# A fused windowed-attention and PReLU kernel: the mask of four head pairs added by TensorE, and slices y and h moved ahead in the first token tile

## The chip, the cores and the metric

The kernel runs on one core of one Trainium2 chip. The metric is the device time of one execution, in microseconds (us). Before the change the median of three runs is 894.59 us (893.28 to 896.59).

## The reference

Windowed causal attention over 8 batches of 8 heads, 576 positions, 64 dims a head (heads 0 to 3 with a plain window of 32, heads 4 to 7 with every fourth key of 128), whose output is 4608 tokens of 512 features; then a feed-forward layer with a PReLU:

```python
scores = scale * np.matmul(q, k.transpose(0, 1, 3, 2))
scores = np.where(masks[None, :, :, :], scores, -1000000000.0)
scores = scores - np.max(scores, axis=-1, keepdims=True)
attn = np.exp(scores)
attn = attn / (np.sum(attn, axis=-1, keepdims=True) + 1e-09)
x = np.matmul(attn, v).transpose(0, 2, 1, 3).reshape(4608, 512)
h = x @ w_in                                   # 512 x 2048
g = np.maximum(h, 0.0) + alpha * np.minimum(h, 0.0)
return g @ w_out                               # 2048 x 512
```

## The kernel before, in words

**Attention.** Two heads are one `Pair`; pair p is batch p // 4, heads 2(p % 4) and the next. A pair goes through `scores` (72 small products on TensorE into two PSUM banks of 5 and 4 blocks of 64 keys), `maxima` (VectorE, twice: scale and add the mask into SBUF at L194, reduce to the negative maximum at L197), `exponentials` (ScalarE, nine of 128x64 at L204, from SBUF, each with its sum), `divisions` and `turns` (VectorE: sum, reciprocal, product, 32x32 transposes into `pt`, L211 to L219), `values` (76 small products, L232, into two banks `o`), and `highs` (ScalarE) and `lows` (VectorE), which write `o` as a rounded part and a remainder into `x`.

**Feed-forward.** Each factor is kept as a high and a low part, and each term is three products of 128x128 by 128x512: high by high, high by low, low by high (weight part first). `ffn_h` of a slice f of 128 of the 2048 columns is 12 products into one bank `h` (L341). `ffn_relu` (ScalarE, L349 and L350) takes both halves of the PReLU, `ffn_sum` (VectorE, L355) joins them, `ffn_high` (ScalarE, L368) and `ffn_low` (VectorE, L373) split the result g, and `ffn_y` is 12 products into four banks `y` (L388), three for each.

**Weights.** They arrive as 64-bit floats. A `Conversion` of one slice is a magnitude (ScalarE, L308), four word operations (VectorE, L314 to L320), a high part (ScalarE, L326) and a low part (VectorE, L329). The list `wq` sets the order of the slices ((0, f) is a slice of the first matrix, (1, f) of the second), and `taken` how many conversions are begun at the end of each step.

**Staging.** Pairs 0 to 3 make the first token tile (tile 0 is 512 tokens, all of batch 0 but 64); a start-up loop over s takes them and pair 4's scores. Then a loop over n = 0 to 5 runs the first six slices of tile 0 (called slice n below) beside pairs 5 to 7, and ends with tile 0's partial sums copied out of the y banks and stored (`ob`, L398 and L400). Tile 1's 16 slices follow (slice 6 is its first), then the rest of tile 0, tile 2, and a paired stage for the other tiles.

**What sets the order.** Nothing is scheduled by a planner: all five engines run what the program text says, in that order, so an instruction that waits holds up everything behind it on its engine. All loads and stores are issued by SP, in program order. Eight PSUM banks are handed out in turn: four, called a, for h, o and the scores of pairs from 5 on, and four, called y, for the scores of pairs 0 to 4 and then for y.

## Time and profile before

| | before |
|---|---|
| median of three runs | 894.59 us |
| profiled execution, device time | 895.02 us |
| its span | 892.9 us |
| TensorE busy | 853.4 us (96%) |
| VectorE / ScalarE / GpSimd busy | 561.3 / 394.3 / 46.9 us |
| granted TensorE clock, mean | 0.98 |

The profile is of one execution on the hardware. PE is TensorE, DVE VectorE, ACT ScalarE, POOL GpSimd, SP the engine that issues DMAs. A row of the timeline gives a start, a duration, engine, line, operation, `out<-in` by the program's names with partitions x elements, and in brackets the engine's idle time just before, with what ended it. The profile leaves buffer numbers out, so that all pairs, slices and weights have like names and are told apart by their place in the engine's order. PEclk is the granted clock as a share of full speed.

### The profile page before, as it was taken

To read this page: it belongs to the slowest core of one execution; us is meant where nothing else is said; L and a number is where in the kernel's file an instruction comes from. 1 tells how busy PE (TensorE), PEld (TensorE's weight loads), DVE (VectorE), ACT (ScalarE), POOL (GpSimd) and SP (SyncE) were. 2 spreads that over 40 slices of the span, in tenths; PEclk is the share of its full clock that TensorE was granted. 3 is DMA by queue.
4 is the path that set the end of the run, shared out by engine and by line. 5 is a ranking of instruction groups with operands and counts; after the bars stand their busy time and mean duration, and the time that the engine had idled before them with its cause. 6 is when DMAs were issued, how large, how long until landed. Compare 5 with 4: busy or idle time off the path is not lost.

```text
span 892.9 us, 19710 instructions
## 1 busy us (share of the span) xinstructions
PE 853.4 (96%) x8048; PEld 706.5 (79%) x8048; DVE 561.3 (63%) x964; ACT 394.3 (44%) x1118; POOL 46.9 (5%) x52
## 2 busy tenths in 40 slices
PE   4668999999999999999999999999999999999998
PEld 4556888888888788888888878888788888888886
DVE  6988799976767677675437655764366537304721
ACT  5566466542533444464336442653255226204600
POOL 0000000020223350000000000000000000000000
PEclk9669999999999999999999999999999999999999
DMA  9612245216889965565556555655365466436631
GB/s 344 219 59 94 86 151 174 80 47 193 253 273 334 301 201 175 188 190 162 156 166 193 173 178 174 195 162 162 96 192 158 148 179 194 124 98 172 180 128 47
DMA packets 101448, 151.81 MB, mean 170 GB/s; under 512 B 8432, under 2 KB 47344, under 8 KB 101360
## 3 DMA queue, kind: packets, MB, share of 16 engines
q1 hardware_dynamic: 101360, 150.58, 54.9%
q8 instruction: 63, 1.03, 0.5%
q14 instruction: 25, 0.20, 0.1%
HBM read 116.99 MB, written 33.55 MB: 169 GB/s over the span
## 4 chain that ended last, share of the span: by engine, by line
PE 94%; DVE 2%; issue 2%; ACT 1%; DMA 0%; SPq 0%; DVEq 0%; ACTq 0%
PE y L676 30%; PE h L341 15%; PE pA L538 15%; PE y L388 15%; PE pC L538 7%; PE o L232 5%; PE pB L538 4%; PE s L186 3%; ACT w_dt.float L204 1%; DMA ws<-w_in 0%; DVE pt L219 0%; DVE w_dt.float L213 0%; DVE w_dt.float32r L329 0%; DVE nm L197 0%; DVE wa L318 0%
## 5 line engine op out<-in xcount | busy, mean ns | idle before, releaser
L341 PE MATMUL h<-x,w_dt.float32r 128*128 128x512 f32 x576 | 144.4, 400 | 1.6 <-issue 1.6
L388 PE MATMUL y<-g,w_dt.float32r 128*128 128x512 f32 x576 | 138.4, 389 | 0.0
L341 PEld LDWEIGHTS h<-x,w_dt.float32r 128*128 128x128 f32 x576 | 109.6, 193 | 25.2 <-issue 1.8
L388 PEld LDWEIGHTS y<-g,w_dt.float32r 128*128 128x128 f32 x576 | 108.0, 188 | 22.5
L676 PE MATMUL y<-gp,ring_w 128*128 128x512 f32 x480 | 112.3, 390 | 0.0
L676 PEld LDWEIGHTS y<-gp,ring_w 128*128 128x128 f32 x480 | 89.7, 188 | 18.9
L676 PE MATMUL y<-gp,ring_xA 128*128 128x512 f32 x444 | 103.8, 390 | 0.0
L676 PEld LDWEIGHTS y<-gp,ring_xA 128*128 128x128 f32 x444 | 83.0, 188 | 17.5
L204 ACT ACTIVATE pr<-pr,nm 128x64 f32<-128x64 f32 x216 | 72.2, 336 | 47.2 <-DVE nm L197 47.2
L580 ACT COPY stage<-pA 128x512 f32<-128x512 f32 x72 | 42.3, 587 | 105.2 <-PE pA L538 105.2
L606 DVE TENSOR_TENSOR gp<-n,gp 128x512 fp32r<-128x512 f32 x96 | 63.1, 683 | 0.0
L368 ACT CAST g<-m 128x512 fp32r<-128x512 f32 x48 | 29.7, 619 | 75.4 <-DVE m L363 69.2
L598 DVE SCALAR_TENSOR_TENSOR n<-n,bal,stage 128x512 f32<-128x512 f32 x72 | 53.9, 748 | 13.6 <-ACT n L594 12.8
L538 PE MATMUL pA<-parts_w,ring_w 128*128 128x512 f32 x234 | 57.7, 390 | 0.7 <-ACT raw_xA L268 0.7
L602 ACT CAST gp<-n 128x512 fp32r<-128x512 f32 x96 | 56.6, 615 | 1.8 <-DVE n L598 1.8
L538 PE MATMUL pA<-parts_w,ring_xA 128*128 128x512 f32 x228 | 56.2, 390 | 0.5 <-ACT raw_xB L268 0.5
L676 PE MATMUL y<-gp,ring_g 128*128 128x512 f32 x228 | 54.5, 391 | 0.0
L699 DVE TENSOR_TENSOR ob<-y,py 128x512 f32<-128x512 f32 x24 | 16.4, 690 | 57.8 <-PE y L676 57.8
L538 PEld LDWEIGHTS pA<-parts_w,ring_w 128*128 128x128 f32 x234 | 43.9, 188 | 9.9 <-ACT raw_xA L268 0.8
L594 ACT ACTIVATE n<-stage 128x512 f32<-128x512 f32 x72 | 45.6, 633 | 12.5 <-DVE stage L587 11.9
L538 PEld LDWEIGHTS pA<-parts_w,ring_xA 128*128 128x128 f32 x228 | 42.7, 188 | 9.5 <-ACT raw_xB L268 0.6
L676 PEld LDWEIGHTS y<-gp,ring_g 128*128 128x128 f32 x228 | 42.5, 188 | 9.1
(97 smaller groups left out, 1147.3 us busy)
## 6 DMA issues: line engine op xcount, KB each, us to landing
ring_w<-wS SPq DMA_DIRECT2D x68, 256.0 KB, 2.9
ring_xA<-wS SPq DMA_DIRECT2D x67, 256.0 KB, 2.9
ring_w<-wO SPq DMA_DIRECT2D x40, 256.0 KB, 2.7
ring_xA<-wO SPq DMA_DIRECT2D x37, 256.0 KB, 2.7
out<-ob SPq DMA_DIRECT2D x36, 256.0 KB, 2.9
ring_g<-wS SPq DMA_DIRECT2D x33, 256.0 KB, 2.9
wO<-w_dt.float32r SPq DMA_DIRECT2D x32, 256.0 KB, 5.0
wS<-wc SPq DMA_DIRECT2D x16, 512.0 KB, 3.7
```

The source lines that it names most:

```text
L204: nc.scalar.activation(out=self.pr[:, r, :], in_=self.pr[:, r, :], func=AF.Exp, bias=self.nm[:, r:r + 1], scale=1.0, accum_out=self.sm[:, ...
L232: nc.tensor.matmul(self.po[u][e * D:(e + 1) * D, a:z, :], lhsT=self.v[rows, i, :], rhs=self.pt[rows, a * BK + (BQ if i else 0):z * BK - (B ...
L341: nc.tensor.matmul(ms[t, f], lhsT=weight(0, a, f)[:, c * P:(c + 1) * P], rhs=half(t, c)[:, e, :], start=(c == 0 and n == 0), stop=(c == NC ...
L368: nc.scalar.copy(out=g[:, 0, :], in_=ms[t, f])
L388: nc.tensor.matmul(ys[t][c], lhsT=weight(1, a, f)[:, c * P:(c + 1) * P], rhs=g[:, e, :], start=(first and n == 0), stop=(last and n == 2),)
L538: nc.tensor.matmul(to, lhsT=w[:, (2 * a + c) * P:(2 * a + c + 1) * P], rhs=part_of(name, e)[:, c * TT:(c + 1) * TT], start=start and c == ...
L580: nc.scalar.copy(out=self.s(n), in_=self.A)
L594: nc.scalar.activation(out=self.m[n], in_=self.at(n), func=AF.Relu, scale=-1.0)
L598: nc.vector.scalar_tensor_tensor(out=self.m[n], in0=self.m[n], scalar=bal[:, f:f + 1], in1=self.at(n), op0=ALU.mult, op1=ALU.add)
L602: nc.scalar.copy(out=self.g(n)[:, 0], in_=self.m[n])
L606: nc.vector.tensor_tensor(out=g[:, 1], in0=self.m.pop(n), in1=g[:, 0].bitcast(F32), op=ALU.subtract)
L676: nc.tensor.matmul(ys2[tt], lhsT=w[:, k * P:(k + 1) * P], rhs=g[:, e], start=j == 0 and n == 0, stop=j == GF - 1 and n == 2)
```

## The change

Three edits, in program order.

**The mask.** For pairs 1 to 4 the mask is added in PSUM: ahead of the 72 products of the scores TensorE multiplies a 128x128 identity (`unit_r`) by the mask (`added`, 320 and 256 columns), and the scores accumulate on top. L194 goes for these pairs; the maximum is reduced straight from PSUM and then scaled by a small `tensor_scalar_mul`, and the exponentials read PSUM and scale there. The identity is made by GpSimd at the program's start, and ScalarE casts it and the two masks.

**The weights.** Slice (0, 3) comes ahead of (1, 1), and of the loop's steps the first begins two conversions, where before the second did.

**The loop over n.** `ffn_y` of slice n - 1 and `ffn_h` of slice n + 2 come ahead of the pair's `values` (before: h of slice n + 1 behind them, y at the end of the step). The relus of slice n + 2 come directly behind g's high part, ahead of the exponentials, and its sum directly behind g's low part.

```diff
@@ -5,6 +5,7 @@
 import concourse.tile as tile
 from concourse import mybir
 from concourse._compat import with_exitstack
+from concourse.masks import make_identity
 
 F32 = mybir.dt.float32
 F32R = mybir.dt.float32r
@@ -120,6 +121,11 @@
     taken = 2 * S + vsize
     spare_pr = [rooms[i][:, taken:taken + HB * BK].rearrange("p (r k) -> p r k", r=HB) for i in range(2)]
     spare_a = [rooms[i][:, taken:taken + DM].bitcast(U32) for i in (2, 3)]
+    added_all = const.tile([P, NMASK + 2, BK], F32R, tag="xC0", name="added")
+    added = {kind: added_all[:, kind:kind + HB] for kind in (PLAIN, DILATED)}
+    unit_r = added_all[:, NMASK:].rearrange("p j k -> p (j k)")
+    unit = rooms[0][:, taken + HB * BK:taken + HB * BK + P]
+    make_identity(nc, unit)
 
 
     cells = {}
@@ -154,6 +160,7 @@
             self.id = f"{b}_{c}"
             self.pr = spare_pr[p % 2] if b < 2 else pr0
             self.room = rooms[c] if b < 2 else None
+            self.onto = 1 <= p <= NC
             self.sm = sums[p % 2]
 
         def load_qk(self):
@@ -177,6 +184,11 @@
 
 
             self.ps = [bank(self.banks, [P, n, BK], f"s_{self.id}_{i}") for i, n in enumerate((CUT0, HB - CUT0))]
+            if self.onto:
+                for i, (a, z) in enumerate(((0, CUT0), (CUT0, HB))):
+                    nc.tensor.matmul(
+                        self.ps[i], lhsT=unit_r, rhs=added[self.mask][:, a:z],
+                        start=True, stop=False, skip_group_check=True)
             for j in range(HB):
                 for u in range(2):
                     for e in range(2):
@@ -185,25 +197,30 @@
                             self.k[rows, None, :BQ].broadcast_to([D, 2, BQ]))
                         nc.tensor.matmul(
                             self.ps[j // CUT0][m * BQ:(m + 1) * BQ, j % CUT0, :], lhsT=self.q[rows, n * BQ:(n + 1) * BQ],
-                            rhs=keys, start=True, stop=True)
+                            rhs=keys, start=not self.onto, stop=True, skip_group_check=self.onto)
 
         def maxima(self, between=()):
             between = list(between)
             self.nm = sml.tile([P, HB], F32, tag="nm", name=f"nm_{self.id}")
             for i, (a, z) in enumerate(((0, CUT0), (CUT0, HB))):
-                nc.vector.scalar_tensor_tensor(
-                    out=self.pr[:, a:z], in0=self.ps[i], scalar=SCALE, in1=mask_sb[:, self.mask + a:self.mask + z],
-                    op0=ALU.mult, op1=ALU.add)
+                if not self.onto:
+                    nc.vector.scalar_tensor_tensor(
+                        out=self.pr[:, a:z], in0=self.ps[i], scalar=SCALE, in1=mask_sb[:, self.mask + a:self.mask + z],
+                        op0=ALU.mult, op1=ALU.add)
                 nc.vector.tensor_reduce(
-                    out=self.nm[:, a:z], in_=self.pr[:, a:z], axis=mybir.AxisListType.X, op=ALU.max, negate=True)
+                    out=self.nm[:, a:z], in_=self.ps[i] if self.onto else self.pr[:, a:z],
+                    axis=mybir.AxisListType.X, op=ALU.max, negate=True)
+                if self.onto:
+                    nc.vector.tensor_scalar_mul(self.nm[:, a:z], self.nm[:, a:z], SCALE)
             for op in between:
                 op()
 
         def exponentials(self, a=0, z=HB):
             for r in range(a, z):
                 nc.scalar.activation(
-                    out=self.pr[:, r, :], in_=self.pr[:, r, :], func=AF.Exp,
-                    bias=self.nm[:, r:r + 1], scale=1.0, accum_out=self.sm[:, r:r + 1],
+                    out=self.pr[:, r, :], in_=self.ps[r // CUT0][:, r % CUT0, :] if self.onto else self.pr[:, r, :],
+                    func=AF.Exp, bias=self.nm[:, r:r + 1], scale=SCALE if self.onto else 1.0,
+                    accum_out=self.sm[:, r:r + 1],
                 )
 
         def divisions(self):
@@ -770,8 +787,9 @@
 
 
     wq = [(0, 0), (0, 1), (1, 0)]
-    for f in range(1, NF):
-        wq += [(0, f + 1), (1, f)] if f + 1 < NF else [(1, f)]
+    wq += [(0, 2), (0, 3), (1, 1), (0, 4), (1, 2), (0, 5), (1, 3), (1, 4), (1, 5)]
+    for f in range(CUT, NF):
+        wq += [(0, f), (1, f)]
     order.update({w: i for i, w in enumerate(wq)})
     loads, convs = list(wq), list(wq)
 
@@ -804,8 +822,10 @@
     pairs[2].load_v()
     pairs[3].load_v()
     pairs[0].scores()
+    before = conversion()
+    nc.scalar.copy(out=unit_r, in_=unit)
+    nc.scalar.copy(out=added[PLAIN], in_=mask_sb[:, PLAIN:PLAIN + HB])
     pairs[1].scores()
-    before = conversion()
     for op in before.words():
         op()
     before.high()
@@ -833,6 +853,8 @@
             ffn_h(0, 0, 0, 2)
         u.turns()
         later = conversion()
+        if s == 0:
+            nc.scalar.copy(out=added[DILATED], in_=mask_sb[:, DILATED:DILATED + HB])
         if s + 2 <= NC:
             pairs[s + 2].scores()
         if s:
@@ -859,7 +881,7 @@
     load()
     late, now = [w], [conversion()]
 
-    taken = [1, 2, 1, 1, 1, 2] + [1, 1, 2, 1, 1, 1, 2, 1, 1, 2, 1, 2, 1]
+    taken = [2, 1, 1, 1, 1, 2] + [1, 1, 2, 1, 1, 1, 2, 1, 1, 2, 1, 2, 1]
 
     def ahead():
         while taken and len(convs) - taken[0] < len(loads):
@@ -869,29 +891,31 @@
         scored = pairs[NC + 1 + n] if n + 1 < NC else None
         valued = pairs[NC + n] if n < NC else None
         if n == 0:
-            for f in range(2):
-                ffn_sum(*slices[f])
+            ffn_sum(*slices[0])
+            ffn_sum(*slices[1])
             valued.divisions()
             valued.turns()
-        elif n > 1:
-            ffn_sum(*slices[n])
         if scored:
             scored.scores()
+        if n:
+            ffn_y(*slices[n - 1])
+        if n + 2 <= CUT:
+            ffn_h(*slices[n + 2])
         if valued:
             valued.values()
-        if n:
-            ffn_h(*slices[n + 1])
         ffn_high(*slices[n])
+        if n + 2 <= CUT:
+            ffn_relu(*slices[n + 2])
         if scored:
             scored.maxima()
             scored.exponentials(0, 5)
         ffn_low(*slices[n])
+        if n + 2 < CUT:
+            ffn_sum(*slices[n + 2])
         if valued:
             valued.highs()
         if scored:
             scored.exponentials(5)
-        if n:
-            ffn_relu(*slices[n + 1])
         for w in now:
             for op in w.words():
                 op()
@@ -906,8 +930,6 @@
             w.high()
         late, now = now, [conversion() for _ in range(taken.pop(0))]
         ahead()
-        if n:
-            ffn_y(*slices[n - 1])
 
     score_at, value_at = {}, {}
     for p in range(2 * NC, AHEAD):
```

Three places where the order changes. First TensorE, around `values` of pair 7 (o_3_1 and o_3_0; w_0 is the name of a weight slice of either matrix). Before:

```order
L341 MATMUL h_3_1046<-x_0_338,w_0_dt.float32r 128x512 x6
L341 MATMUL h_3_1046<-x_1_571,w_0_dt.float32r 128x512 x6
L388 MATMUL y_0_0_951<-g_1_909,w_0_dt.float32r 128x512 x3
L388 MATMUL y_0_1_952<-g_1_909,w_0_dt.float32r 128x512 x3
L388 MATMUL y_0_2_953<-g_1_909,w_0_dt.float32r 128x512 x3
L388 MATMUL y_0_3_954<-g_1_909,w_0_dt.float32r 128x512 x3
L232 MATMUL o_3_1_1121<-pt_3_1101,w_2_dt.float_91 64x32 x2
L232 MATMUL o_3_0_1120<-pt_3_1101,w_2_dt.float_91 64x64 x2
```

And now:

```order
L405 MATMUL y_0_0_890<-g_2_1109,w_0_dt.float32r 128x512 x3
L405 MATMUL y_0_1_891<-g_2_1109,w_0_dt.float32r 128x512 x3
L405 MATMUL y_0_2_892<-g_2_1109,w_0_dt.float32r 128x512 x3
L405 MATMUL y_0_3_893<-g_2_1109,w_0_dt.float32r 128x512 x3
L358 MATMUL h_5_1166<-x_0_350,w_0_dt.float32r 128x512 x6
L358 MATMUL h_5_1166<-x_1_587,w_0_dt.float32r 128x512 x6
L249 MATMUL o_3_1_1180<-pt_3_1149,w_2_dt.float_91 64x32 x2
L249 MATMUL o_3_0_1179<-pt_3_1149,w_2_dt.float_91 64x64 x2
```

The y ahead of pair 7's values is of slice 2 where it was of slice 1, the h of slice 5 where it was of slice 3, and the two have changed places.

Then VectorE in the same step, from pair 7's transpose on (g_3 is the low part of slice 3, m_3 and m_5 are sums, w_2_dt.float_91 the words of a weight slice, x_1 pair 7's low parts, and the last row but one step the weight's low part). Before:

```order
L219 STREAM_TRANSPOSE pt_3_1101<-w_2_dt.float_89 128x576
L355 SCALAR_TENSOR_TENSOR m_3_1081<-m_3_1081,nal,h_3_1046 128x512
L373 TENSOR_TENSOR g_3_1173<-m_3_1081,g_3_1173 128x512
L314 TENSOR_SCALAR w_2_dt.float_91<-w_2_dt.float_91 128x512
L316 TENSOR_SCALAR w_2_dt.float_91<-w_2_dt.float_91 128x512
L318 SCALAR_TENSOR_TENSOR w_2_dt.float_91<-w_1_dt.uint_94,w_2_dt.float_91 128x512
L320 SCALAR_TENSOR_TENSOR w_2_dt.float_91<-w_1_dt.uint_94,w_2_dt.float_91 128x512
L273 TENSOR_TENSOR x_1_572<-o_3_0_1120,x_1_572 128x2x112
L273 TENSOR_TENSOR x_1_1072<-o_3_0_1120,x_1_1072 128x2x32
L273 TENSOR_TENSOR x_1_572<-o_3_1_1121,x_1_572 128x2x112
L273 TENSOR_TENSOR x_1_1072<-o_3_1_1121,x_1_1072 128x2x32
L329 TENSOR_TENSOR w_0_dt.float32r<-w_2_dt.float_90,w_0_dt.float32r 128x512
```

And now:

```order
L236 STREAM_TRANSPOSE pt_3_1149<-w_2_dt.float_89 128x576
L390 TENSOR_TENSOR g_3_1219<-m_3_961,g_3_1219 128x512
L372 SCALAR_TENSOR_TENSOR m_5_1221<-m_5_1221,nal,h_5_1166 128x512
L331 TENSOR_SCALAR w_2_dt.float_91<-w_2_dt.float_91 128x512
L333 TENSOR_SCALAR w_2_dt.float_91<-w_2_dt.float_91 128x512
L335 SCALAR_TENSOR_TENSOR w_2_dt.float_91<-w_1_dt.uint_94,w_2_dt.float_91 128x512
L337 SCALAR_TENSOR_TENSOR w_2_dt.float_91<-w_1_dt.uint_94,w_2_dt.float_91 128x512
L290 TENSOR_TENSOR x_1_588<-o_3_0_1179,x_1_588 128x2x112
L290 TENSOR_TENSOR x_1_1126<-o_3_0_1179,x_1_1126 128x2x32
L290 TENSOR_TENSOR x_1_588<-o_3_1_1180,x_1_588 128x2x112
L290 TENSOR_TENSOR x_1_1126<-o_3_1_1180,x_1_1126 128x2x32
L346 TENSOR_TENSOR w_0_dt.float32r<-wa_3_1003,w_0_dt.float32r 128x512
```

The sum ahead of the weight's words is that of slice 5, whose h is the one just ahead of pair 7's values on TensorE; before it was that of slice 3.

Last ScalarE at the end of the loop (g_0_4 and g_0_5 are the high parts of slices 4 and 5, m_1_0 and h_1_0 the relus of tile 1's first slice, L326 or L343 a weight's high part). Before:

```order
L368 CAST g_0_4_1223<-m_0_4_1180 128x512
L349 ACTIVATE m_0_5_1226<-h_0_5_1210 128x512
L350 ACTIVATE h_0_5_1210<-h_0_5_1210 128x512
L326 CAST w0_0_dt.float32r_84<-wa0_6_1194 128x512
L308 ACTIVATE w2_2_dt.float32_90<-w0_1_dt.uint32_92 128x512
L368 CAST g_0_5_1264<-m_0_5_1226 128x512
L349 ACTIVATE m_1_0_1267<-h_1_0_1251 128x512
L350 ACTIVATE h_1_0_1251<-h_1_0_1251 128x512
```

And now:

```order
L385 CAST g_0_4_1268<-m_0_4_1111 128x512
L366 ACTIVATE m_1_0_1270<-h_1_0_1255 128x512
L367 ACTIVATE h_1_0_1255<-h_1_0_1255 128x512
L343 CAST w2_0_dt.float32r_86<-wa1_5_1240 128x512
L325 ACTIVATE w2_2_dt.float32_90<-w0_1_dt.uint32_92 128x512
L385 CAST g_0_5_1295<-m_0_5_1221 128x512
```

The relus of tile 1's first slice, the weight's high part and a magnitude behind them now stand ahead of the high part of slice 5.

## Rows read from the trace of the kernel before

**Rows 1.** The page: the span, each engine's busy time, and the chain of waits by engine.

```profile
span 892.9 us, 19710 instructions
PE 853.4 (96%) x8048; PEld 706.5 (79%) x8048; DVE 561.3 (63%) x964; ACT 394.3 (44%) x1118; POOL 46.9 (5%) x52
...
PE 94%; DVE 2%; issue 2%; ACT 1%; DMA 0%; SPq 0%; DVEq 0%; ACTq 0%
```

**Rows 2.** Windows by stage: from and to (us), length, then busy us and instructions of PE, PEld, DVE, ACT and POOL, the granted clock PEclk, the DMA share and GB/s.

```profile
53.00:90.00 37.00, 29.82 (x521) 25.34 (x522) 32.99 (x71) 23.49 (x88) 0.00 (x0) 0.79 0.23 73
90.00:112.00 22.00, 22.00 (x99) 18.23 (x98) 16.59 (x29) 10.63 (x21) 0.00 (x0) 1.00 0.26 93
112.00:160.00 48.00, 48.00 (x214) 39.75 (x213) 45.52 (x82) 30.23 (x54) 0.00 (x0) 1.00 0.47 152
...
200.00:893.00 693.00, 684.71 (x6091) 565.59 (x6082) 394.55 (x642) 280.94 (x780) 40.97 (x42) 1.00 0.59 179
```

**Rows 3.** Timeline of TensorE in the loop over n. In order: values of pair 4, scores of pair 7, values of pairs 6 and 7, h of slices 4 and 5, y of slices 3 and 6.

```profile
53.21 2.34 PE L232 MATMUL o<-pt,w_dt.float 32*64 32x32 f32 x76 [3.36 <-DVE pt L219]
...
69.83 1.21 PE L186 MATMUL s<-w_dt.float 64*32 64x64 f32 x72
70.97 1.35 PE L232 MATMUL o<-pt,w_dt.float 32*64 32x32 f32 x76
...
81.47 1.82 PE L232 MATMUL o<-pt,w_dt.float 32*64 32x32 f32 x76 [3.47 <-issue]
83.22 4.10 PE L341 MATMUL h<-x,w_dt.float32r 128*128 128x512 f32 x12
...
89.88 2.88 PE L341 MATMUL h<-x,w_dt.float32r 128*128 128x512 f32 x12
92.60 2.88 PE L388 MATMUL y<-g,w_dt.float32r 128*128 128x512 f32 x12
...
108.92 2.88 PE L388 MATMUL y<-g,w_dt.float32r 128*128 128x512 f32 x12
```

**Rows 4.** Windows of 1 us of TensorE alone: from and to, length, busy us and instructions, granted clock, DMA share, GB/s.

```profile
81.00:82.00 1.00, 0.53 (x35) 1.00 0.00 0
...
84.00:85.00 1.00, 1.00 (x4) 0.50 0.00 0
```

**Rows 5.** Timelines of the start-up: ScalarE's first high part of a weight, VectorE's maxima of pair 1 (the first two of four rows) with that pair's first exponential on ScalarE, a small VectorE operation, and GpSimd's work, much later.

```profile
9.18 0.62 ACT L326 CAST w_dt.float32r<-wa 128x512 fp32r<-128x512 f32 x1 [2.40 <-DVE wa L320]
...
17.15 0.48 DVE L194 SCALAR_TENSOR_TENSOR w_dt.float<-s,mask_sb 128x320 f32<-128x320 f32 x1
17.67 0.49 DVE L197 TENSOR_REDUCE nm<-w_dt.float 128x5 f32<-128x320 f32 x1
...
18.19 0.35 ACT L204 ACTIVATE w_dt.float<-w_dt.float,nm 128x64 f32<-128x64 f32 x1 [2.85 <-DVE nm L197]
...
14.64 0.17 DVE L211 TENSOR_SCALAR rs<-sums 128x9 f32<-128x9 f32 x1
...
182.52 3.27 POOL L440 TENSOR_TENSOR wsum_xB<-wsum_xB 128x256 f32<-128x256 f32 x4
```

**Rows 6.** Timeline of VectorE in the loop: maxima of pair 5, the first word of a conversion, pair 4's low parts, maxima of pair 6; then the sum of slice 2, pair 6's low parts, a weight's low part, the low part of slice 5, and the last copy of tile 0's sums.

```profile
53.08 0.45 DVE L194 SCALAR_TENSOR_TENSOR w_dt.float<-s,mask_sb 128x320 f32<-128x320 f32 x1
...
55.36 0.42 DVE L314 TENSOR_SCALAR w_dt.float<-w_dt.float 128x512 f32<-128x512 f32 x1
...
57.61 0.88 DVE L273 TENSOR_TENSOR x<-o,x 128x288 fp32r<-128x288 f32 x3
...
60.95 0.45 DVE L194 SCALAR_TENSOR_TENSOR w_dt.float<-s,mask_sb 128x320 f32<-128x320 f32 x1
...
68.81 0.71 DVE L355 SCALAR_TENSOR_TENSOR m<-m,nal,h 128x512 f32<-128x512 f32 x1
...
77.48 1.36 DVE L273 TENSOR_TENSOR x<-o,x 128x224 fp32r<-128x224 f32 x4
78.75 0.68 DVE L329 TENSOR_TENSOR w_dt.float32r<-wa,w_dt.float32r 128x512 fp32r<-128x512 f32 x1
...
95.52 0.69 DVE L373 TENSOR_TENSOR g<-m,g 128x512 fp32r<-128x512 f32 x1 [0.85 <-ACT g L368]
...
109.88 0.69 DVE L398 COPY ob<-y 128x512 f32<-128x512 f32 x1 [3.41 <-DMA part<-ob]
```

**Rows 7.** Timeline of ScalarE: the two relus of a slice, the high part of a weight, the first of two magnitudes, and the high part of a slice's g, late in the loop.

```profile
98.30 0.60 ACT L349 ACTIVATE m<-h 128x512 f32<-128x512 f32 x1 [2.81 <-PE h L341]
98.80 0.59 ACT L350 ACTIVATE h<-h 128x512 f32<-128x512 f32 x1
99.31 0.60 ACT L326 CAST w_dt.float32r<-w_dt.float 128x512 fp32r<-128x512 f32 x1
99.82 0.68 ACT L308 ACTIVATE wa<-w_dt.uint 128x512 f32<-128x512 f32 x1
...
100.97 0.60 ACT L368 CAST g<-m 128x512 fp32r<-128x512 f32 x1
```

**Rows 8.** Waits from 40 to 112 us: engine and line, waited for, us in all, times, longest.

```profile
DVE m L355 <- ACT h L350: 4.8, 5, 1.9
...
DVE g L373 <- ACT g L368: 2.4, 3, 0.9
...
DVE w_dt.float L194 <- PE s L186: 1.2, 1, 1.2
```

## The prediction

> **What bounds the kernel now.** I read the page first, then the windows by stage, then the timelines of the three engines over the first 112 us. By the page TensorE is busy 853.4 of 892.9 us and 94% of the chain that ends last [rows 1], so only the time in which TensorE stands, or runs at the lower of its two clock levels, can be won. The windows say where that is: from 90 to 160 us it is busy without a gap at full clock, and from 200 us on it stands 693.00 - 684.71 = 8.3 us in all; from 53 to 90 us it stands 37.00 - 29.82 = 7.2 us at a mean clock of 0.79 [rows 2]. That stretch is the loop over n, where the third edit works. VectorE is the busiest other engine there, 32.99 of 37.00 us; its idle time comes in single waits for scores (1.2 us) and for parts of g (2.4 us) [rows 8], and ScalarE's relus wait for TensorE's h. The loop is thus a relay between engines, and the question is how long one round of it is after the change. From 90 us on TensorE has no gap to swallow a delay, so what arrives late at tile 1's first y moves the end by as much.
>
> **The mask, pairs 1 to 4.** For each pair two rows of L194 go (0.48 and 0.41 us), two small scalings come (0.17 us for a like operation [rows 5]), and the 576 identity columns cost TensorE two products, 0.5 us at full clock and twice that at half (below: 0.227 us for 512 columns), while it waits for transposes anyway. On the path lies what stands ahead of a pair's first exponential: before, 17.15 to 18.19 = 1.04 us; after, the reduction (0.49), the scaling (0.17) and a hand-over of some 0.03 us, 0.70 in all. Three pairs (1 to 3) feed each other in the start-up, pair 4's maxima lie beside other work: 3 x 0.34 = 1.0 us earlier at pair 4's transpose. Bounds: nothing (the exponentials, now reading PSUM, or the later scores of pairs 2 to 4, give it back) to 1.5 us (the second scaling and L194 count too); I take 1.0, the rows' own difference. The casts of identity and masks, about 0.9 us together by the 0.62 us of a 128x512 one, fit in the 2.40 us for which ScalarE stands before its first high part at 9.18 us, if the identity is there by 9.18 - 0.9 = 8.3 us. GpSimd's rows show 3.27 / 4 = 0.82 us for a 128x256 operation [rows 5], which puts the identity at about 2 us.
>
> No row shows GpSimd's first use of a routine at a program's start. The Trainium skill ("GPSIMD Engine Reference", 2.1 Instruction dispatch) says that the first call of a freshly loaded routine pays about 6 us for its code: an estimate from that page puts the identity at 7 to 7.5 us, still before 8.3, and the sum stays.
>
> **The conversions.** The new order of weights and the two conversions begun a step earlier move one set of four words (57.61 - 55.36 = 2.25 us [rows 6]) from step 2 of the loop to step 1; the total is the same, and the loads that SP issues are the same in number, in the new order.
>
> **The loop, round by round.** VectorE's queue sets it. Its pieces, start to start: a pair's maxima and g's low part, 55.36 - 53.08 = 2.28; a set of words, 2.25; the tail (low parts of x, a weight's low part, division, transpose) 60.95 - 57.61 = 3.34; low parts of x for a later pair 78.75 - 77.48 = 1.27; a weight's low part 0.68; a sum 0.71 [rows 6]. TensorE's: 12 products 92.60 - 89.88 = 2.72, so 0.227 each, and 10 of them 2.27 [rows 3]. ScalarE's: two relus 98.80 + 0.59 - 98.30 = 1.09; a weight's high part 0.51, a magnitude (100.97 - 99.82) / 2 = 0.57, g's high part 0.60 [rows 7].
>
> Step 0 starts on VectorE at 53.08 - 1.0 = 52.1 and takes 2.28 + 0.71 + 2.25 + 3.34, to 60.7. Step 1: maxima and low part to 63.0. Now comes the sum of slice 3, before a step later. It needs h of slice 3, which stands behind the scores of pair 6 and y of slice 0: the scores' bank is free after slice 2's sum at 55.1, and 55.1 + 1.2 + 2.72 + 2.72 + 1.09 = 62.8 us, just in time at full clock. At the lower clock it is late by an amount w. Then 0.71 + 4.50 (two sets of words) + 3.34: 71.5 + w. Step 2: 2.28 + 0.71 + 2.25 + 1.27 + 0.68 bring the low part of weight (1, 2) at 78.7 + w. Here is the new wait: y of slice 2 now stands ahead of pair 7's values, and its third product needs this low part. TensorE has reached it at about 74.4 + w, since pair 6's transpose came at 71.5 + w and its values take 1.35 at full clock and a little more behind the wait; so it stands some 4 us with h of slice 5 and pair 7's values queued behind. Then the round closes: y's other ten products 2.27, h of slice 5 2.72, relus 1.09, the sum 0.71, behind which the words are queued in VectorE's order, 2.25, low parts of x 1.27, weight (1, 3)'s low part 0.68, together 11.0 us: 89.7 + w + s, where s is the price of a slow stretch of TensorE after its wait. There y of slice 3 has its third product, at which TensorE has stood again. Before, that product was at 92.60 + 0.45 = 93.05 and waited for nothing. But what follows is longer than it was: y's rest 2.27, h of slice 6 2.72, its relus 1.09, which now stand ahead of slice 5's high part on ScalarE, with a weight's high part 0.51 and a magnitude 0.57, then that high part 0.60. Slice 5's low part comes at 89.7 + 7.8 = 97.5 + w + 2s; before it came at 95.52, so 2.0 + w + 2s late. VectorE's idle time behind it swallows some 0.4 (of the 4.8 us in which it waits for relus [rows 8]), and the last copy of tile 0's sums, ready at 109.88 + 0.69 = 110.57, had 108.92 + 9 x 0.227 = 110.96 as its due time at tile 1's first y, 0.4 more [rows 3, 6]. TensorE there loses 1.2 + w + 2s, and nothing behind takes it back [rows 2].
>
> **The clock.** Pair 7's values came after 3.47 us of standing; the granted clock, 1.00 in the window at 81 us, was 0.50, the 1.2 GHz level, at 84 us [rows 4]. The values took 1.82 us against pair 6's 1.35, and h of slice 4 4.10 against slice 5's 2.88 [rows 3]: s = 0.47 + 1.22 = 1.7. In step 1 pair 4's values (2.34 against 1.35) show that the clock is low too, after a wait of 3.36; with the 0.2 us to spare w is 1.7 - 0.2 = 1.5. From below, both are zero; from above, a third slow stretch at the last copies adds 1.7.
>
> The Trainium skill ("TensorE: Matmul & The Clock Gate", Part 1: The HAM clock gate) calls the ramp's penalty less than 1% of a typical span and variable from run to run, and advises not to fit a specific count. By that advice w and s would be left out, and the sum would be +1.2 us; the rows show 1.7 after one wait, and I keep them.
>
> **Sum.** 1.2 + 1.5 + 2 x 1.7 = +6.1 us on the profiled execution's 895.02: 901.1. The median of the runs is 0.43 below that execution: 900.7 us. The forecast's own range is 895.3 (no slow stretch, start-up gain 1.5) to 903.4 (a third slow stretch, start-up gain 0).
>
> **Rivals.**
> - The relay gets shorter, faster than before: with y and h ahead of the values TensorE finds work where it stood, h comes two slices ahead, and the relus and sums never hold VectorE. Then its waits for scores and for g (1.2 + 2.4 us [rows 8]) go, and the start-up gives 1.0: 894.59 - 4.6 = 890.0. For it: 7.2 us of standing are there to be won, and slice 3's h is due within 0.2 us by the sum above. Against: the weights' low parts stand behind the words in VectorE's queue. It decides if y of slice 2 finds weight (1, 2)'s low part before 76 us.
> - The clock stays high through both waits: w and s are zero, 895.02 + 1.2 - 0.43 = 895.8, no change that can be told. For it: the clock held through the window at 81 us, behind a wait of 3.47 us. Against: one microsecond later it fell.
> - The identity is late, slower: from 8.3 us on, each us moves ScalarE's first high part, the first exponentials and the whole start-up. GpSimd 3 us late gives 903.7. For it: no row has GpSimd at work in the start-up; against: all its rows are short.
>
> **How the numbers follow.** A difference of under 0.5% (4.5 us, 890.1 to 899.1) can't be told from no change by a measurement of this kernel. The forecast has 0.56, of which 0.10 lie below 899.1; the steady clock 0.18, all no change; the shorter relay 0.18, of which 0.12 lie below 890.1 and 0.06 above; the late identity 0.08, slower. Faster 0.12, same 0.10 + 0.18 + 0.06 = 0.34, slower 0.46 + 0.08 = 0.54. The range 890.0 to 904.0 leaves out half of the shorter relay and the upper ends of forecast and late identity, under 0.2.
>
> **What would show it.** Right: TensorE stands 3 us or more ahead of the third product of y of slices 2 and 3, each followed by a microsecond at clock 0.50; pair 4's transpose about 1 us earlier; slice 5's low part 2 us late or more, and a gap of TensorE before tile 1's first y. Wrong: h of slice 5 and pair 7's values begin before VectorE has written weight (1, 2)'s low part; TensorE stands less than 7.2 us in the loop; slice 5's low part no later than 95.5; or ScalarE's first high part later than 9.2 us.

## The result and the profile after

The changed kernel takes 899.95 us (median of 7 runs, 897.7 to 901.53); the kernel before, run beside it, 894.59. The ratio is 1.0053, with a 95% interval of 1.0035 to 1.007: slower by 0.5%, 0.75 us under the forecast of 900.7 and inside both of its ranges. The profiled execution has a span of 896.9 us, 4.0 more than before.

The page of the changed kernel, with the lines that answer to [rows 1]:

```profile
span 896.9 us, 19730 instructions
PE 856.0 (95%) x8056; PEld 703.7 (78%) x8056; DVE 558.8 (62%) x964; ACT 394.8 (44%) x1121; POOL 47.4 (5%) x54
...
PE 90%; DVE 6%; ACT 2%; issue 1%; DMA 1%; SPq 0%; ACTq 0%; DVEq 0%
```

TensorE's share of the chain fell from 94% to 90%, and VectorE's rose from 2% to 6%: TensorE now stands for it. Where, two of the windows of [rows 2] show (columns as there):

```profile
53.00:90.00 37.00, 27.41 (x406) 20.67 (x400) 29.81 (x65) 21.03 (x77) 0.00 (x0) 0.89 0.19 59
90.00:112.00 22.00, 18.81 (x71) 14.78 (x72) 13.98 (x25) 8.62 (x16) 0.00 (x0) 0.88 0.23 71
```

TensorE stands 9.6 us from 53 to 90 us, where it was 7.2, and 3.2 us from 90 to 112 us, where it had no gap at all. The waits of the changed kernel from 40 to 125 us name the pairs of engines (columns as in [rows 8]):

```profile
PE y L405 <- DVE w_dt.float32r L346: 8.9, 3, 4.2
DVE m L372 <- ACT h L367: 8.3, 4, 5.0
```

The first row is a wait that the kernel before did not have: y stands three times, 8.9 us in all, for a weight's low part. TensorE's timeline shows the places: h of slice 4 in two pieces, values of pair 6, y of slice 2 in two pieces, h of slice 5, values of pair 7, y of slice 3 in two pieces, and much later tile 1's first y, again in two:

```profile
66.26 0.73 PE L358 MATMUL h<-x,w_dt.float32r 128*128 128x512 f32 x2 [1.26 <-DVE x L290]
67.29 4.14 PE L358 MATMUL h<-x,w_dt.float32r 128*128 128x512 f32 x10 [0.30 <-DVE w_dt.float32r L346]
71.36 1.35 PE L249 MATMUL o<-pt,w_dt.float 32*64 32x32 f32 x76
72.64 0.73 PE L405 MATMUL y<-g,w_dt.float32r 128*128 128x512 f32 x2
77.56 4.15 PE L405 MATMUL y<-g,w_dt.float32r 128*128 128x512 f32 x10 [4.18 <-DVE w_dt.float32r L346]
81.55 2.89 PE L358 MATMUL h<-x,w_dt.float32r 128*128 128x512 f32 x12
84.36 1.35 PE L249 MATMUL o<-pt,w_dt.float 32*64 32x32 f32 x76
85.64 0.74 PE L405 MATMUL y<-g,w_dt.float32r 128*128 128x512 f32 x2
90.57 4.63 PE L405 MATMUL y<-g,w_dt.float32r 128*128 128x512 f32 x10 [4.19 <-DVE w_dt.float32r L346]
...
111.78 2.58 PE L405 MATMUL y<-g,w_dt.float32r 128*128 128x512 f32 x6 [2.10 <-ACT ob L417]
114.52 2.16 PE L405 MATMUL y<-g,w_dt.float32r 128*128 128x512 f32 x6 [0.15 <-ACT ob L417]
```

Both times two products of y run, and the third stands 4.2 us; the ten that follow take 4.15 and 4.63 us, where ten at full clock take 2.56 (those of y of slice 5, from 104.41 us on). Tile 1's first y ends at 116.68 us; before it ended at 108.92 + 2.88 = 111.80 [rows 3]. Of these 4.9 us the end shows 4.0.

VectorE's timeline has the other half of the round (sum of slice 4, low parts of pair 6, the first of two weights' low parts; then the sum of slice 5 and a weight's low part; then slice 5's low part):

```profile
72.65 0.75 DVE L372 SCALAR_TENSOR_TENSOR m<-m,nal,h 128x512 f32<-128x512 f32 x1 [1.20 <-ACT h L367]
...
75.56 1.35 DVE L290 TENSOR_TENSOR x<-o,x 128x224 fp32r<-128x224 f32 x4
76.82 0.68 DVE L346 TENSOR_TENSOR w_dt.float32r<-wa,w_dt.float32r 128x512 fp32r<-128x512 f32 x1
...
85.65 0.75 DVE L372 SCALAR_TENSOR_TENSOR m<-m,nal,h 128x512 f32<-128x512 f32 x1 [5.03 <-ACT h L367]
...
89.83 0.68 DVE L346 TENSOR_TENSOR w_dt.float32r<-wa,w_dt.float32r 128x512 fp32r<-128x512 f32 x1
...
100.81 0.69 DVE L390 TENSOR_TENSOR g<-m,g 128x512 fp32r<-128x512 f32 x1 [6.84 <-ACT g L385]
```

The low part of weight (1, 2) ends at 77.50 us and y goes on at 77.56; that of (1, 3) ends at 90.51 and y goes on at 90.57. Between the two, VectorE itself stood 5.03 us for the relus of slice 5, whose h stood behind y. So TensorE waits for VectorE, and VectorE, through ScalarE's relus, for TensorE: that is the round.

### The profile page after: what moved, and what is told of

Read it like the earlier page. It is cut to its first block, busy times and chain, and to the rows that moved or that the text cites. A ratio compares the mean times of both kernels' runs of the same rounds, so it can differ in the third digit from the quotient of the medians.

```text
span 896.9 us, 19730 instructions
## 1 busy us (share of the span) xinstructions
PE 856.0 (95%) x8056; PEld 703.7 (78%) x8056; DVE 558.8 (62%) x964; ACT 394.8 (44%) x1121; POOL 47.4 (5%) x54
## 4 chain that ended last, share of the span: by engine, by line
PE 90%; DVE 6%; ACT 2%; issue 1%; DMA 1%; SPq 0%; ACTq 0%; DVEq 0%
PE y L693 29%; PE pA L555 15%; PE h L358 14%; PE y L405 14%; PE pC L555 7%; PE o L249 4%; PE pB L555 4%; PE s L198 3%; ACT w_dt.float L220 1%; DMA ws<-w_in 1%; DVE w_dt.float32r L346 1%; DVE x L290 1%; DVE m L372 0%; DVE w_dt.float L335 0%; DVE wa L335 0%
## 5 line engine op out<-in xcount | busy, mean ns | idle before, releaser
L405 PE MATMUL y<-g,w_dt.float32r 128*128 128x512 f32 x576 | 145.2, 402 | 11.1 <-DVE w_dt.float32r L346 8.9
L405 PEld LDWEIGHTS y<-g,w_dt.float32r 128*128 128x128 f32 x576 | 110.6, 194 | 36.7 <-DVE w_dt.float32r L346 10.2
L358 PEld LDWEIGHTS h<-x,w_dt.float32r 128*128 128x128 f32 x576 | 108.2, 190 | 27.2 <-issue 1.9
```

The source lines that it names most:

```text
L358: nc.tensor.matmul(ms[t, f], lhsT=weight(0, a, f)[:, c * P:(c + 1) * P], rhs=half(t, c)[:, e, :], start=(c == 0 and n == 0), stop=(c == NC ...
L405: nc.tensor.matmul(ys[t][c], lhsT=weight(1, a, f)[:, c * P:(c + 1) * P], rhs=g[:, e, :], start=(first and n == 0), stop=(last and n == 2),)
```

## The experiments

Each time is the median beside runs of the kernel before, and each ratio is to those.

**The mask alone** (the changed kernel with the weights' order, the counts and the loop of the kernel before) **and the loop alone** (the kernel before with the three of the changed one):

```diff
-    wq += [(0, 2), (0, 3), (1, 1), (0, 4), (1, 2), (0, 5), (1, 3), (1, 4), (1, 5)]
...
-    taken = [2, 1, 1, 1, 1, 2] + [1, 1, 2, 1, 1, 1, 2, 1, 1, 2, 1, 2, 1]
+    taken = [1, 2, 1, 1, 1, 2] + [1, 1, 2, 1, 1, 1, 2, 1, 1, 2, 1, 2, 1]
...
```

(Lines of the first kernel against the changed one; its loop's body, put back as before the change, is left out here.)

Expected of the mask alone: 

> The mask by identity products alone, with the weights' order and the loop over n of the kernel before. Theory (the loss is the loop's, the mask is a gain in the start-up): in the changed kernel pair 4's transpose came 3.3 us earlier than before though its first DMA landed 1 us later; carried to the end that is 894.6 - 3.3 = 891.3, between 890 and 892.5. Rival (the mask costs: exponentials from PSUM, scores that wait for the casts): 894.6 or more, and most of the 5.4 us lost. Rival (the gain is swallowed at the loop's next wait): 894 to 895.

Expected of the loop alone: 

> The weights' order and the loop of the changed kernel alone, with the mask added on VectorE as before. Theory: all of the loss and none of the gain, 899.95 + 3.3 = 903.3, between 902 and 905. Rival (the mask is what costs): 894 to 896. If the parts don't add up, the sum of both parts' differences will not be +5.4.

Measured: the mask alone 893.77 us, ratio 0.9985 (0.9974 to 0.9997); the loop alone 903.75 us, ratio 1.0092 (1.0077 to 1.0108). The loss is that of the loop and the weights' order together: that rival falls which put it on the mask. But the mask alone lies above the 890 to 892.5 of its theory: its gain came out at 0.15% in the old loop and, by the difference of 1.0092 and 1.0053, at about 0.4% in the new one. So the 3.3 us of the one profile don't show in the median of the old loop. The two parts' differences, -1.2 and +8.8 us, add up to 7.6 and not to 5.4: the parts depend on each other.

**The mask alone, a second profiled execution.** Expected: 

> The same kernel as the mask alone, one more execution with its profile. That one's profiled execution was 890.5 us, its median 893.8. Theory (the clock's fall in the start-up comes or not by chance): an execution near the median shows clock 0.50 at 38 to 45 us, where that profile showed 1.00, and starts the loop 1.5 to 2.5 us later. Rival (the first load's landing decides): the clock is the same and the first magnitude starts later than 6.8 us.

Measured: one execution of 892.29 us. Neither theory held: the loop began at the same time in both (pair 4's transpose at 48.87 and 49.09 us), with pair 3's values at 1.35 us in both. The executions differ in the loop, by how much of the work behind the waits ahead of pairs 5 and 7 is slow. Values of pair 5 and h of slice 2, first in the execution of 890.51 us and then in that of 892.29:

```profile
57.84 2.04 PE L249 MATMUL o<-pt,w_dt.float 32*64 32x32 f32 x76 [3.49 <-issue]
59.80 3.87 PE L358 MATMUL h<-x,w_dt.float32r 128*128 128x512 f32 x12
```

```profile
57.61 2.35 PE L249 MATMUL o<-pt,w_dt.float 32*64 32x32 f32 x76 [4.07 <-issue]
59.89 4.96 PE L358 MATMUL h<-x,w_dt.float32r 128*128 128x512 f32 x12
```

The granted clock from 61 to 63 us was 0.67 and 1.00 in the first and 0.50 in the second; behind pair 5's wait the second falls back by 1.2 us and behind pair 7's by 0.9. So a difference of some 2 us between two executions of one kernel goes with the clock, and a single profile can flatter a kernel by as much.

**The weights' low parts ahead of the sum.**

```diff
         ffn_low(*slices[n])
+        for w in late:
+            w.low()
         if n + 2 < CUT:
             ffn_sum(*slices[n + 2])
...
-        for w in late:
-            w.low()
         if scored:
             scored.divisions()
```

Expected: 

> The changed kernel with one edit on VectorE's queue: a step's weight low parts stand directly behind g's low part, ahead of the sum of slice n + 2, the conversion's words and the pair's low parts. Theory (y of slices 2 and 3 stand for a weight's low part queued behind sum, words and x's low parts): both waits of 4.2 us shrink under 1 us, the clock doesn't fall behind them, and the time comes to 889 to 893. Rival (VectorE's total work bounds the loop, the order within a step doesn't matter): 899 to 901. Rival (only the clock after a wait costs): 896 to 898.

Measured: 888.8 us, ratio 0.9938 (0.9925 to 0.9951), faster than both kernels, and 0.2 us below the theory's 889 to 893. VectorE does the same work; only its order within a step changed. TensorE's timeline from y of slice 2 to y of slice 3, and its place at tile 1's first y:

```profile
71.94 3.59 PE L405 MATMUL y<-g,w_dt.float32r 128*128 128x512 f32 x12
75.36 2.88 PE L358 MATMUL h<-x,w_dt.float32r 128*128 128x512 f32 x12
79.73 1.35 PE L249 MATMUL o<-pt,w_dt.float 32*64 32x32 f32 x76 [1.48 <-issue]
81.01 3.00 PE L405 MATMUL y<-g,w_dt.float32r 128*128 128x512 f32 x12
...
102.11 2.44 PE L405 MATMUL y<-g,w_dt.float32r 128*128 128x512 f32 x6 [4.50 <-ACT ob L417]
```

Neither of the two y is broken, and neither is followed by slow work. Y of slice 3 ends at 84.0 us where it ended at 95.2. Not all of these 11 us reach the end: at tile 1's first y TensorE now stands 4.5 us for tile 0's copies, and that y is slow (2.44 us for its first six products).

**Work for TensorE in the waits.** Ahead of y of slices 2 and 3 fifteen products were added whose result is overwritten:

```diff
...
+        if n in (3, 4):
+            ffn_idle(*slices[n + 2], 15)
         if n:
             ffn_y(*slices[n - 1])
```

Expected: 

> The changed kernel with 15 products of 128x128 by 128x512 (3.4 us at full clock) more on TensorE ahead of y of slice 2 and again ahead of y of slice 3; their result is overwritten. TensorE stood 4.2 us there, so they fit. Theory (a wait is followed by a slow stretch worth 1.7 us, twice): the clock stays at 1.00 behind both waits and the time falls by 1.5 to 3.4 us, 896.5 to 898.5. Rival (the clock is a symptom, the relay is bound by VectorE): 899 to 901. Rival (the added products get in the way): above 901.5.

Measured: 895.51 us, ratio 1.0012 (0.9997 to 1.0028). The granted clock stayed at 1.00 from 60 us through both waits, and the ten products took 2.57 and 2.58 us:

```profile
73.45 3.69 PE L365 MATMUL h<-x,w_dt.float32r 128*128 128x512 f32 x15
...
78.68 2.57 PE L411 MATMUL y<-g,w_dt.float32r 128*128 128x512 f32 x10 [1.08 <-DVE w_dt.float32r L346]
...
90.10 2.58 PE L411 MATMUL y<-g,w_dt.float32r 128*128 128x512 f32 x10 [0.78 <-DVE w_dt.float32r L346]
```

Thirty products without use made the kernel 4.4 us faster (3.7 by the difference of the two ratios), so the slow stretches are a price of their own and no mere symptom. The gain is above the expected 1.5 to 3.4; in the profiled execution h of slice 4 was at full clock too (2.57 us for its ten products against 4.14), which the added work, coming behind it, doesn't explain: it was so too in the profile of the kernel with tile 1's relus moved (2.56 us), whose program is the changed one's up to there. The part that the edit can be credited with is 4.15 + 4.63 - 2.57 - 2.58 = 3.6 us.

**y at the end of the step again.**

```diff
-        if n:
-            ffn_y(*slices[n - 1])
         if n + 2 <= CUT:
             ffn_h(*slices[n + 2])
...
         ahead()
+        if n:
+            ffn_y(*slices[n - 1])
```

Expected: 

> The changed kernel with y of slice n - 1 back at the end of the step, behind the pair's values; h, relus and sum stay two slices ahead. Theory (what costs is that y, waiting for a weight's low part, has h and the pair's values queued behind it): the waits of 4.2 us ahead of y of slices 2 and 3 go, and the time falls to that of the mask with the old loop, 892 to 896. Rival (the early relus and sums on ScalarE and VectorE cost): 899 to 901.

Measured: 891.23 us, ratio 0.9957 (0.9943 to 0.997). A little better than expected, and the rival falls: with h, relus and sums two slices ahead and y behind the values, the kernel is faster than before. What cost in the change was the place of y. In this execution y of slices 1 to 3 runs whole, and TensorE's largest wait in the loop is 2.4 us, for h of slice 5 and a weight's low part:

```profile
80.04 2.56 PE L358 MATMUL h<-x,w_dt.float32r 128*128 128x512 f32 x10 [2.38 <-DVE w_dt.float32r L346]
...
83.81 3.01 PE L405 MATMUL y<-g,w_dt.float32r 128*128 128x512 f32 x12
```

**The sum behind the low parts.**

```diff
         ffn_low(*slices[n])
-        if n + 2 < CUT:
-            ffn_sum(*slices[n + 2])
...
         for w in late:
             w.low()
+        if n + 2 < CUT:
+            ffn_sum(*slices[n + 2])
```

Expected: 

> The changed kernel with the sum of slice n + 2 on VectorE behind the words, the pair's low parts and the weights' low parts. Theory (the round closes because the words stand behind a sum that waits for an h which itself stands behind the waiting y): VectorE's wait of 5.0 us ahead of slice 5's sum no longer holds the words, TensorE's second wait falls from 4.2 us to 1 to 2 us, the first by 1 to 2 us; 893 to 897. Rival (words and x's low parts alone are what the weight's low part waits for, the sum is small): 898 to 900.

Measured: 905.05 us, ratio 1.0102 (1.0085 to 1.0119): 8 us above the theory's range and 5 above the rival's, a miss of both. The second wait did fall (2.04 us, from 4.19) and the first too (3.49), but a new one came at the scores:

```profile
56.41 1.08 PE L198 MATMUL s<-w_dt.float 64*32 64x64 f32 x32 [4.17 <-DVE m L372]
...
70.32 0.65 PE L198 MATMUL s<-w_dt.float 64*32 64x64 f32 x32 [3.39 <-DVE m L372]
```

The sum reads h in PSUM, and the next pair's scores take that bank in turn. A sum that comes later gives its bank back later, and the scores, y, h and values behind them wait. The expectation took the sum for a stage that produces g and left out that it also frees a bank.

**The relus of tile 1's first slice behind slice 5's high part.**

```diff
-        if n + 2 <= CUT:
+        if n + 1 == CUT:
+            ffn_relu(*slices[CUT])
+        if n + 2 < CUT:
             ffn_relu(*slices[n + 2])
```

Expected: 

> The changed kernel with the relus of tile 1's first slice behind the high part of slice 5 on ScalarE. Theory: the low part of slice 5, which waited 6.8 us on ScalarE, comes some 6 us earlier, tile 0's copies no longer hold tile 1's first y (2.1 + 0.15 us of standing go); 897 to 898.5. Rival (the copies are late for another reason, the words ahead of them): 899.5 to 900.5.

Measured: 895.38 us, ratio 0.9999 (0.9982 to 1.0015); 4.6 us faster than the changed kernel, where 1.5 to 3 were expected. Slice 5's low part and tile 1's first y in its timelines:

```profile
94.81 0.69 DVE L390 TENSOR_TENSOR g<-m,g 128x512 fp32r<-128x512 f32 x1 [1.15 <-ACT g L385]
```

```profile
108.35 2.88 PE L405 MATMUL y<-g,w_dt.float32r 128*128 128x512 f32 x12
```

The low part comes at 94.8 us instead of 100.8 and y is whole, and ends 116.68 - 111.23 = 5.4 us earlier. The expectation counted only the standing at that y (2.25 us). It left out the 0.5 us of standing at y of slice 5, and that the first y was slow besides (clock 0.50 from 113 to 114 us): its two pieces took 116.68 - 111.78 = 4.9 us, of which 0.15 are standing, and 2.88 is what such a y takes at full clock.

**The two last parts apart.** Expected of the mask with the new weights' order and the old loop: 

> The mask and the new order of weights (two conversions begun in the first step) with the old loop's body. Theory (the weights' order moves four words by a step and costs nothing by itself): 892.5 to 895. Rival (the earlier second conversion delays pair 6 by 2.25 us and is part of the loss): 896 to 898.

Expected of the mask with the old loop and the low parts ahead: 

> The mask alone with the old loop, and the weights' low parts directly behind g's low part as in the kernel with the low parts ahead. Theory (in the old loop y stands at the end of a step, so that nothing waits for a weight's low part): as the mask alone, 892.5 to 894.5. Rival (low parts ahead are worth the same in any loop, the moves of y and h give nothing): 887 to 890.

Measured: 890.82 us, ratio 0.9951 (0.9932 to 0.997), and 892.58 us, ratio 0.9971 (0.9957 to 0.9985). The new order of weights, with two conversions in the first step, is no part of the loss: in the old loop it is worth about 3 us beside the mask alone, more than expected. TensorE's wait ahead of pair 7's values, 3.48 us with the mask alone, is 2.02 there; the rest of the 3 us was not traced to a place.

```profile
79.29 1.81 PE L249 MATMUL o<-pt,w_dt.float 32*64 32x32 f32 x76 [2.02 <-issue]
```

This run also parts the weights' order from the loop's body. From 0.9951 to the changed kernel's 1.0053 only the body differs: the moves of y, h, relus and sums cost 1.0%, some 9 us, as they stand. With the low parts ahead they come to 0.9938, an interval that overlaps with that of 0.9951. So of the 0.6% that the kernel with the low parts ahead gains, 0.5% is there with the old loop's body, and that the moves themselves gain anything is not shown.

Low parts ahead give the old loop 0.14% with overlapping intervals, no change that can be told; this was with the old order of weights. It fits that their worth depends on y standing ahead of h.

**Two tries beyond the kernel with the low parts ahead.** The copies of tile 0's sums ahead of two conversions' words:

```diff
+        if n == CUT:
+            ffn_y(*slices[n - 1])
         if n <= SECOND - 2:
...
+            if n == CUT:
+                while ended:
+                    ended.pop()()
```

Expected: 

> The kernel with the weights' low parts ahead, and besides the copies of tile 0's sums directly behind slice 6's sum and the weight's low part, ahead of two conversions' words (y of slice 5 is written ahead of them; TensorE's order is the same). In the kernel without it TensorE stood 4.5 + 0.3 us for the copies at tile 1's first y. Theory (they are late for the words ahead of them on VectorE and ScalarE): the standing falls to 1.5 us or less, 884.5 to 887. Rival (the copies' own buffers wait 3.4 us for the stores, so the last one stays late; slice 6's parts come later in exchange): 888 to 890.

Expected of the relus of tile 1's first slice behind slice 5's high part, there: 

> The kernel with the weights' low parts ahead, and besides the relus of tile 1's first slice behind the high part of slice 5. Theory (there the copies are late for the words, not for slice 5's high part, which waits only 1.75 us): 888 to 889.5, no change to the kernel without it. Rival (the relus hold the copies up as in the changed kernel, where taking them back gave 4.6 us): 884 to 886.

Measured: 890.51 us, ratio 0.9952 (0.9934 to 0.997), and 890.34 us, ratio 0.9952 (0.9933 to 0.9971): neither is better than the 888.8 without them, and both lie above the ranges of their theories. With the relus moved back the wait for the copies is the same 4.5 us, as the theory had it: there the words hold the copies. With the copies ahead of the words the wait for them is gone, and its place is taken by one for slice 6's low part, which now stands behind the copies on VectorE, and the work behind it is slow:

```profile
98.64 0.39 PE L405 MATMUL y<-g,w_dt.float32r 128*128 128x512 f32 x1
102.61 5.06 PE L405 MATMUL y<-g,w_dt.float32r 128*128 128x512 f32 x11 [3.58 <-DVE g L390]
```

## Why the prediction was right, and where its terms were off

**The mechanism** held at the places named. y of slices 2 and 3 wait at their third product, 4.18 us where some 4 were forecast and then 4.19, and go on within 0.06 us of the end of the weight's low part. The round between the two, forecast as 11.0 + 1.7 = 12.7 us, took 90.57 - 77.56 = 13.0. Slice 5's low part, the first row named as a sign, came at 100.81 us, 5.3 later than before (2 or more expected), and TensorE had its gap ahead of tile 1's first y. That the low part's place in VectorE's queue decides is shown by the kernel that only moved it.

**The start-up** was undersized: 1.0 us forecast, with 1.5 as its upper bound. Pair 4's transpose came at 49.08 us against 52.38, 3.3 us earlier. Transposes of pairs 3 and 4, then 18 products of h between them, in the changed kernel and in the kernel before:

```profile
37.07 0.78 DVE L236 STREAM_TRANSPOSE pt<-w_dt.float 128x576 f32<-128x576 f32 x1
...
49.08 0.78 DVE L236 STREAM_TRANSPOSE pt<-w_dt.float 128x576 f32<-128x576 f32 x1
...
39.83 4.39 PE L358 MATMUL h<-x,w_dt.float32r 128*128 128x512 f32 x18
```

```profile
37.85 0.78 DVE L219 STREAM_TRANSPOSE pt<-w_dt.float 128x576 f32<-128x576 f32 x1
...
52.38 0.78 DVE L219 STREAM_TRANSPOSE pt<-w_dt.float 128x576 f32<-128x576 f32 x1
...
41.62 5.75 PE L341 MATMUL h<-x,w_dt.float32r 128*128 128x512 f32 x18
```

Two things are in this. Up to pair 3's transpose (37.07 against 37.85) the gain is 0.78, although ScalarE's first magnitude waited until 7.16 us for its load, 1.06 us longer than before; together 1.84, or 0.61 for each pair, where 0.34 were forecast. The step that failed is the one that gave the exponentials no part but a possible loss: read from PSUM, nine of them and their sums take less. First exponential of pair 2 and the operation behind the ninth, in the changed kernel and in the kernel before:

```profile
25.97 0.31 ACT L220 ACTIVATE w_dt.float<-s,nm 128x64 f32<-128x64 f32 x1 [1.31 <-DVE nm L214]
...
28.59 0.80 ACT L285 CAST x<-o 128x288 fp32r<-128x288 f32 x3
```

```profile
25.80 0.35 ACT L204 ACTIVATE w_dt.float<-w_dt.float,nm 128x64 f32<-128x64 f32 x1 [2.81 <-DVE nm L197]
...
28.80 0.72 ACT L268 CAST x<-o 128x288 fp32r<-128x288 f32 x3
```

2.62 against 3.00 us: 0.38 more for each pair, and 0.34 + 0.38 = 0.72 bounds the 0.61 seen. The rest, 2.5 us between pair 3's and pair 4's transposes, is the clock: pair 3's values took 1.35 us (2.35 before) and the 18 products of h 4.39 (5.75). This part is not the mask's for certain: of the twelve profiled executions with the mask eight have 12.0 us between the two transposes, as here, and four 13.5 to 14.7; the two without it have 14.5 and 14.3. Medians put the mask's worth at 1.2 us in the old loop, near the forecast 1.0, and at 3.8 in the new one.

**w**, the delay by a low clock in step 1, had about the right size (1.2 us measured, 1.5 forecast) and the wrong place. Slice 3's sum was forecast late if the clock was low; the clock was full there, and step 1 took 69.09 - 58.31 = 10.8 us, the forecast with w at zero. The delay came a step later: h of slice 4 stood 1.26 us for a bank that pair 5's low parts free and 0.30 for a weight's low part, both queued behind two sets of words in step 1, then ran at clock 0.50, and slice 4's sum waited 1.20 us for its relus. The forecast had the two sets of words but not what stands behind them. And w comes only when the clock falls there: in the kernel with tile 1's relus moved, h of slice 4 was fast, and y of slice 2 went on 27.2 us behind pair 4's transpose, where it took 28.5 in the changed kernel.

**s**, the price of a slow stretch behind a wait, was forecast at 1.7 us, twice. The ten products behind each wait took 4.15 and 4.63 us against 2.57 and 2.58 with work in the waits: 1.6 and 2.1. The granted clock of TensorE, in windows of 1 us behind the first wait (columns as in [rows 4]) and at 113 us:

```profile
77.00:78.00 1.00, 0.44 (x2) 1.00 0.87 336
78.00:79.00 1.00, 1.00 (x4) 0.55 0.29 115
79.00:80.00 1.00, 1.00 (x4) 0.50 0.00 0
...
113.00:114.00 1.00, 1.00 (x4) 0.50 0.99 373
```

The last row is a third slow stretch, at tile 1's first y: 4.9 - 0.15 - 2.88 = 1.9 us. The prediction left it to its upper bound, at 1.7; the sum lacks it. Without w and s the sum would have been +1.2 us, no change that can be told. The Trainium skill ("TensorE: Matmul & The Clock Gate", Part 1: The HAM clock gate) puts the ramp's penalty below 1% of a typical span. By that figure the trace agrees: the two stretches, 3.6 us, are 0.4% of 896.9. As advice to leave them out it would have turned "slower" into "no change".

**The sum.** +6.1 us were forecast; measured are +4.0 in the spans of the profiled executions and +5.4 in the medians. The start-up's gain was 2.3 us too small in the forecast. The loop's loss was forecast as 6.1 + 1.0 = 7.1 and came to 4.9 + 3.3 = 8.2, 1.1 more; the third slow stretch alone is 1.9. And 0.9 came back where TensorE stands in both kernels: from 270 to 310 and from 500 to 540 us it stood 2.9 us before and 2.0 after. 6.1 - 2.3 + 1.1 - 0.9 = 4.0: errors of opposite sign are part of why the number was so near, and that is luck.

**The rivals.** The shorter relay did not happen, and could have: its condition was that y finds the weight's low part, and the kernel that grants it takes 888.8 us against the 890.0 that this rival gave. But most of that gain is there without the moves of y and h (890.82 us with the old loop's body), so it doesn't show that the relay got shorter by this rival's reason. The steady clock did not hold by itself. The late identity did not happen: GpSimd's operation, of which the trace before had no row, is short and early.

```profile
1.01 0.29 POOL masks.py:199 TENSOR_SCALAR_AFFINE_SELECT w_dt.float<-w_dt.float 128x128 f32<-128x128 f32 x1
```

It ended at 1.30 us. Of the 6 us for the first call of a freshly loaded routine, which the Trainium skill ("GPSIMD Engine Reference", 2.1 Instruction dispatch) states, this trace shows nothing. ScalarE's first high part came at 10.22 us and not by 9.2, which the prediction had named as a sign against it; the load is the reason there, not the identity, since the magnitude ahead of it waited for its DMA.

What stays open: whether the first load's landing (6.10 us before, 7.16 after, 6.8 to 8.0 in the other kernels with the mask, 6.50 in the loop alone) is later because of the change or by chance; no run was made on it. Its price is below 2 us either way.

## What to carry to other kernels

When a consumer is moved ahead on an engine that runs in order, look up where its last operand stands in the producer's queue, and what has just been queued behind the consumer: here y ahead of h made a ring of TensorE, ScalarE and VectorE, and one line moved on VectorE (the operand's producer ahead of a sum that waits for the same ring) turned 5 us of loss into 6 us of gain. Run the parts of a change apart as well: here 0.5 of the 0.6% came with the mask and the new order of weights in the old loop, and the moves that the loop was rewritten for were not shown to gain. A stage that reads a PSUM bank also gives it back, so moving it later can hold up work that has nothing to do with its result. And each of the two waits of 4.2 us on TensorE was followed by work that took 1.6 or 2.1 us longer.

## What the runs showed of the hardware that was not expected

Exponentials of 128x64 with their sums follow each other at 0.29 us from PSUM and 0.33 from SBUF in this kernel (2.62 and 3.00 us for nine). Two executions of one kernel, the mask alone, differ by some 2 us that go with the granted clock: the wait ahead of pair 5's values (3.49 and 4.07 us) was followed by 2.04 + 3.87 us of work in one and by 2.35 + 4.96 in the other. Products without use, put into two waits, made a kernel 4.4 us faster, more than the 1.5 to 3.4 expected.
